# Turning du, Q and dO by crossbar DMAs instead of on TensorE, with other loads, lags and a reordered end, in a gated attention and FFN gradient

## The chip, the cores and the metric

The kernel runs on one core of one Trainium2 chip. The metric is the device time of one execution in microseconds, and less is better. An "engine" below is one of the core's units: TensorE (PE, with its weight loads listed as PEld), VectorE (DVE), ScalarE (ACT), GpSimd (POOL) and SyncE (SP), which here does nothing but issue DMAs. A "crossbar DMA" is a DMA that writes its data transposed (`dma_start_transpose`).

## The reference

One layer mixes sliding-window attention and a ReLU-gated feed-forward block with a gate per row; the kernel must give its output and the gradients with respect to everything but the feed-forward input. The forward pass, cut to what matters:

```python
# S = 2048 rows, D = 512, 32 heads of 16, window W = 256, F = 1376, all bf16
g = sigmoid((x * gate_w).sum(-1, keepdims=True))
q, k, v = split(x @ wqkv)                      # heads of 16
p = softmax(where(0 <= i - j < 256, q @ k.T / 4, -1e9))
a = (p @ v) @ wo
gate = B_x @ W_gate; gate = gate * (gate > 0)
h = gate * (B_x @ W_up)
b = h @ W_down
out = g * a + (1 - g) * b
# returned: out and, for a given grad_out, the gradients
# of x, wqkv, wo, W_gate, W_up, W_down and gate_w
# (B_x holds the same numbers as x and gets no gradient of its own)
```

## The kernel before

Rows are handled in tiles of 128 (16 of them) and in groups of four tiles (512 rows, index `tg`). Transposed copies, with features on the partitions, have names in T (`hT`, `dgT`, `duT`, `QT`, `dOT`, `KT`, `VT`); row copies have names in `_r` or `rows`. There are three stages.

**Feed-forward stage.** 44 steps run over 11 feature chunks `fc` times 4 row groups `tg`. One turn n of the loop issues `gate` and `up` of step n (matmuls `gps` and `ups`, from which `rg`, `upm` and `hT` come), `dh` of step n-1 (matmul `dhps`, from which `dgT` and `duT` come), then the turns: `turn_h` of step n-1 and `turn_dg` of step n-2 as crossbar DMAs on SP's queue, `turn_du` of step n-3 as four TensorE transposes into PSUM (`ptu`) and a DVE copy; `keep` of step n-3 stores `hT`, `dgT` and `duT` to DRAM from ACT's queue; `weights` of step n-4 multiplies the turned tiles into the weight gradients `wps` and `dps`. The first four turns also turn x (`turn_x`), compute the gate column (`gate_col`), scale grad_out into `db_r` (`db_rows`, four DVE operations per group) and turn that into `db_T` (`turn_db`), on which `dh` depends. Group loads of grad_out, `go_in`, are issued on POOL's queue with two buffers, so the third and fourth wait for `db_rows` of the first two.

**Attention stage.** The order is written out by hand (`manual_schedule`). Units of work run over 4 chunks `c` of 8 heads, 16 row tiles `j`, up to three key tiles `kb` and two halves of four heads: 360 units, one per slot n. In a slot, `front` issues two matmuls for unit n (scores `ST`, and `dPT`, the gradient of the probabilities), Exp on ACT and the mask on POOL, then `gradp` forms `Pd` on DVE; `rowsum` and `flip` handle unit n-2. A flip transposes `Pu` and `Pd`: for units on the diagonal (a third of them, tile `PP`) by a crossbar DMA `p<-PP` on SP's queue, for all others by eight TensorE transposes. Then come pieces of older work (`cd_piece`, which reads the flipped `p`) and, when a running credit of TensorE time allows, `project_parts` of the next row group (matmuls for Q, dO, K, V; `tr_rows`, which turns `QT` and `dOT` into `rows` by TensorE transposes `ptp` and two DVE copies, the first scaled; `tr_kv`, the same for K and V), and background work. SP's queue also carries `spread` and `gather` (`z_d<-QT`, `z<-z_d`: the block-structured operand of the next scores), the turns of weight matrices through DRAM (`wt`), loads `dar` of the attention's output gradient, and the stores of the gradients of q, k, v and of O (`spill`: four DMAs into `dqkv_d` and `O_d`). After the last unit the remaining slots drain what is left; at the end of the stage the operands of the next one are loaded (`early_group`, `late_weights`, `load_group(0)`).

**Final stage.** 16 row tiles: 11 matmuls for b, 4 for a, 22 and 12 for dx (lines L912, L915 and L919), plus one for the gradient of gate_w; a tile's dx is stored by a DMA on POOL's queue.

Within one engine's queue instructions run in the order in which they are written; DMAs on one issuing engine are issued in that order too.

Of the kernel before, what the change touches and what calls it, by code (L numbers as in the profile page):

```python
# [22 lines left out]
def kernel(  # L23
# [64 lines left out]
    dqkv_d = dram.tile([S, 3 * D], BF, name="dqkv_d")  # L88
    O_d = dram.tile([S, D], BF, name="O_d")
# [33 lines left out]
    with ExitStack() as p1, tc.manual_schedule():  # L123
# [25 lines left out]
        nc.sync.dma_start(x_r[:, 0:TPG, :], rows_of(x_d, 0))  # L149
# [4 lines left out]
        load_go(0)  # L154
        load_go(1)
# [3 lines left out]
        nc.scalar.dma_start(Wg_sb[:, :, W0:F], Wg_v[:, :, W0:F])  # L159
        nc.scalar.dma_start(Wu_sb[:, :, W0:F], Wu_v[:, :, W0:F])  # L160
# [24 lines left out]
        def db_rows(tg):  # L185
            for k in range(TPG):
                t = tg * TPG + k
                nc.vector.tensor_scalar(db_r[:, t, :], go_in[tg][:, k, :], omg_all[:, t:t + 1], None, op0=ALU.mult)
            if tg + 2 < NTG:
                load_go(tg + 2)  # L190
# [72 lines left out]
        def dh(k):  # L263
# [4 lines left out]
            k.dgT, k.duT = tile1("dgT"), tile1("duT")  # L268
            nc.vector.tensor_tensor(out=k.dgT[:], in0=dh_sb[:], in1=k.upm[:], op=ALU.mult)
            nc.gpsimd.tensor_tensor(out=k.duT[:], in0=dh_sb[:], in1=k.rg[:], op=ALU.mult)  # L270

        def turn_h(k):
            k.h_r = fp.tile([P, TPG, P], BF, tag="h_r", name="h_r")
            nc.sync.dma_start_transpose(out=k.h_r[:], in_=k.hT[:])

        def turn_dg(k):
            k.dgu_r = fp.tile([P, 2, TPG, P], BF, tag="dgu_r", name="dgu_r")
            nc.sync.dma_start_transpose(out=k.dgu_r[:, 0, :, :], in_=k.dgT[:])

        def turn_du(k):  # L280
            pt = ps1.tile([P, TPG, P], BF, tag="tr", bufs=2, name="ptu")
            for t in range(TPG):
                nc.tensor.transpose(pt[:, t, :], k.duT[:, t * P:(t + 1) * P], ident[:])
# [36 lines left out]
        for n in range(N1 + 6):  # L320
# [47 lines left out]
    if True:  # L368
        st = p3.enter_context(tc.tile_pool(name="attst", bufs=2))
        gwp = p3.enter_context(tc.tile_pool(name="gwp", bufs=2))  # L370
        p3b = ExitStack()
        wq = p3b.enter_context(tc.tile_pool(name="wq", bufs=1))
# [3 lines left out]
        zt = [wq.tile([P, 2, HG, 2 * P], BF, name=f"z{i}") for i in range(ZB)]  # L376
# [8 lines left out]
        def project_parts(c, tg):  # L385
# [25 lines left out]
            def tr_rows():  # L411
                rows = pj.tile([P, 2, TPG, P], BF, tag="rows", name="rows")
                pt = tr("Q", "dO")
                nc.vector.tensor_scalar(rows[:, 0, :, :], pt[:, 0, :, :], scale, None, op0=ALU.mult)
                nc.vector.tensor_copy(rows[:, 1, :, :], pt[:, 1, :, :])
                t4["rows"] = rows

            def tr_kv():
# [3 lines left out]
                for a, lo, eng in ((0, 0, "dve"), (1, 17, "dve")):  # L422
# [3 lines left out]
            return [lambda: mm("Q", 0, "dve"), lambda: mm("dO", 3, "dve"), lambda: mm("K", 1, "dve"),  # L426
                    lambda: mm("V", 2, "dve"), tr_rows, tr_kv]
# [18 lines left out]
        def cd_piece(c, kb, qb, half, last):  # L446
# [12 lines left out]
            if last:  # L459
                nc.scalar.copy(sts[c][0][:, kb, 1:3, :].rearrange("p a (h d) -> p h a d", h=HG),  # L460
# [504 lines left out]
```

## Time and profile before

| what | value |
|---|---|
| median of three runs | 1039.25 us (1038.76 to 1042.58) |
| profiled execution | 1040.05 us, span 1038.3 us |
| mean granted TensorE clock | 0.986 |
| instructions of PE | 11852 matmuls, 982.8 us busy (95% of the span) |
| DVE, ACT, POOL busy | 55%, 46%, 45% |
| DMA traffic | 162.85 MB in 393335 packets, of which 293297 are under 512 B |
| feed-forward stage | 0 to about 283 us |
| attention stage | about 283 to 855 us |
| final stage | about 855 us to the end |

A profile is one execution; its times are microseconds unless marked ns. A row of the timeline gives start, duration, engine, line, operation, the tile written and the tiles read, and in brackets how long the engine stood idle before it and what it then waited for. A row of windows gives the length of a stretch and the busy time of each engine in it, then the granted clock, the mean busy share of the 16 DMA engines and GB/s. Matmuls overlap: a matmul of 128x512 shows 0.38 us, while in an unbroken stream the next one starts 0.22 us after it. So a busy PE need not be a PE at its best, and what a matmul costs is read from the distance between starts.

### The profile page before, as it was taken

The page shows a single profiled execution, that of the slowest core. Times are in us where ns is not written, and L with a number is a line of the kernel's source. Part 1 is how long each engine was busy: PE and PEld are TensorE (multiplying, and loading weights), DVE is VectorE, ACT ScalarE, POOL GpSimd, SP SyncE. Part 2 cuts the span into 40 slices and gives each one's busy share as a digit, 9 for nine tenths or more (in the row PEclk, how much of TensorE's full clock was granted, in tenths as well). Part 3 has the DMA queues.
Part 4 walks back from the last instruction along what each step waited for, and adds up shares of the span by engine and source line. Part 5 has one row for each costly group of instructions (what it writes and reads, how often), then busy time and mean ns, then how long its engine had stood idle before and what let it go on. Part 6 is the DMA issues. An engine that isn't in the chain of part 4 may idle for free.

```text
span 1038.3 us, 28954 instructions
## 1 busy us (share of the span) xinstructions
PE 982.8 (95%) x11852; PEld 634.0 (61%) x11852; DVE 569.8 (55%) x1101; ACT 481.1 (46%) x808; POOL 466.4 (45%) x810
## 2 busy tenths in 40 slices
PE   5799999999989999999999999999999769999997
PEld 3466666566647777677776777766777534444443
DVE  3344444333268888767788677886777502322222
ACT  3323333222147777666677676666667411001000
POOL 2355544344345556655556455565555411211211
PEclk9999999999999999999999999999999879999999
DMA  9557676866555676787767776569869989667740
GB/s 303 90 148 178 179 178 169 205 160 142 136 114 102 123 145 117 154 168 149 143 119 149 163 161 127 132 118 177 143 97 231 266 222 260 158 154 179 187 107 21
DMA packets 393335, 162.85 MB, mean 157 GB/s; under 512 B 293297, under 2 KB 388818, under 8 KB 393202
## 3 DMA queue, kind: packets, MB, share of 16 engines
q1 hardware_dynamic: 368306, 131.30, 60.6%
q10 hardware_dynamic: 21648, 20.13, 6.2%
q0 software_dynamic: 3248, 9.57, 3.0%
q8 instruction: 93, 1.52, 0.6%
q14 instruction: 40, 0.33, 0.1%
HBM read 54.36 MB, written 48.10 MB: 99 GB/s over the span
## 4 chain that ended last, share of the span: by engine, by line
PE 82%; DMA 7%; issue 3%; DVE 3%; ACT 2%; SPq 1%; POOL 1%; ACTq 0%; POOLq 0%; DVEq 0%
PE pt L647 9%; PE wps L298 7%; PE dPT L598 7%; PE ST L596 7%; PE gps L247 4%; PE bps L883 4%; PE dhps L247 4%; PE CD L454 4%; PE dxps L919 3%; PE BA L624 3%; PE dps L300 3%; PE pp L395 3%; PE ups L247 3%; PE dxps L912 3%; PE dxps L915 3%; PE wps L540 3%
## 5 line engine op out<-in xcount | busy, mean ns | idle before, releaser
L615 DVE TENSOR_TENSOR Pd<-Pu,dPT 128x512 bf16<-128x512 bf16 x232 | 158.3, 684 | 55.2 <-POOL Pu L609 34.1
L604 ACT ACTIVATE Pu<-ST 128x512 bf16<-128x512 f32 x232 | 139.5, 601 | 59.2 <-PE ST L596 53.2
L606 POOL TENSOR_SCALAR_AFFINE_SELECT PP<-PP 128x512 bf16<-128x512 bf16 x128 | 81.1, 634 | 160.7 <-ACT PP L604 160.1
L598 PE MATMUL dPT<-z,VT 128*128 128x512 bf16 x360 | 136.5, 379 | 4.1 <-DVE Pd L615 1.6
L596 PE MATMUL ST<-z,KT 128*128 128x512 bf16 x360 | 136.3, 379 | 0.8 <-DMA z<-z_d 0.8
L75 ACT COPY p<-pt 128x1024 bf16<-128x1024 bf16 x116 | 117.4, 1012 | 30.7 <-PE pt L647 30.3
L454 PE MATMUL CD<-rq,p 128*128 128x32 bf16 x1440 | 117.0, 177 | 7.9 <-DMA p<-PP 6.4
L457 PE MATMUL CD<-rq,p 128*128 128x16 bf16 x1440 | 113.7, 169 | 0.0
L261 POOL TENSOR_TENSOR hT<-rg,upm 128x512 bf16<-128x512 bf16 x44 | 50.5, 1148 | 134.5 <-DVE upm L259 114.0
L298 PE MATMUL wps<-dgu_r,x_r 128*128 128x256 bf16 x704 | 106.8, 275 | 2.1 <-DVE wst L77 2.0
L604 ACT ACTIVATE PP<-ST 128x512 bf16<-128x512 f32 x128 | 76.7, 600 | 55.0 <-PE ST L596 48.2
L454 PEld LDWEIGHTS <-p 128*128 128x128 bf16 x1440 | 95.8, 96 | 6.7 <-DMA p<-PP 6.7
L609 POOL TENSOR_SCALAR_AFFINE_SELECT Pu<-Pu 128x512 bf16<-128x512 bf16 x112 | 71.1, 634 | 56.3 <-ACT Pu L604 54.7
L77 DVE COPY p<-pt 128x1024 bf16<-128x1024 bf16 x116 | 79.7, 687 | 28.3 <-PE pt L647 26.8
L615 DVE TENSOR_TENSOR PP<-PP,dPT 128x512 bf16<-128x512 bf16 x128 | 86.6, 677 | 9.9 <-POOL PP L606 9.8
L624 PEld LDWEIGHTS <-Pu 128*128 128x128 bf16 x928 | 68.0, 96 | 37.3 <-issue 10.3
L647 PE MATMUL pt<-ident,Pd 128*128 128x128 bf16 x928 | 90.2, 220 | 0.0
L457 PEld LDWEIGHTS <-p 128*128 128x128 bf16 x1440 | 89.0, 96 | 1.7 <-issue 1.7
L647 PE MATMUL pt<-ident,Pu 128*128 128x128 bf16 x928 | 89.3, 218 | 0.0
L298 PEld LDWEIGHTS <-x_r 128*128 128x128 bf16 x704 | 67.6, 99 | 24.4 <-issue 3.2
L259 DVE SCALAR_TENSOR_TENSOR upm<-rg,ups 128x512 bf16<-128x512 bf16 x44 | 30.2, 687 | 94.0 <-PE ups L247 91.9
L624 PE MATMUL BA<-KV,Pu 128*128 128x33 bf16 x928 | 77.5, 178 | 4.5 <-ACT BAs L630 3.9
(136 smaller groups left out, 2073.8 us busy)
## 6 DMA issues: line engine op xcount, KB each, us to landing
z<-z_d SPq DMA_DIRECT2D x128, 64.0 KB
dar<-da_d SPq DMA_DIRECT2D x28, 256.0 KB
hT_d<-hT ACTq DMA_DIRECT2D x44, 128.0 KB
dgT_d<-dgT ACTq DMA_DIRECT2D x44, 128.0 KB
duT_d<-duT ACTq DMA_DIRECT2D x44, 128.0 KB
dqkv_d<-dqkv_st SPq DMA_DIRECT2D x21, 256.0 KB
hT_g<-hT_d SPq DMA_DIRECT2D x8, 640.0 KB
dgT_g<-dgT_d SPq DMA_DIRECT2D x8, 640.0 KB
```

Source lines behind the costliest of these rows:

```text
L75: nc.scalar.copy(out, in_)
L247: nc.tensor.matmul(out[:], lhsT=w(c), rhs=x(c), start=(c == 0), stop=(c == DC - 1))
L298: nc.tensor.matmul(acc["w"][:, c, :], lhsT=x_r[:, t, c * P:(c + 1) * P], rhs=k.dgu_r[:, :, i, :], start=(go_ and c % 2 == 0), stop=no_, sk ...
L454: nc.tensor.matmul(cd[0][:, h, :], lhsT=p2[:, 0, hh, :], rhs=rq[:, h, 0:2 * Dh], start=cd[1], stop=True, skip_group_check=True)
L457: nc.tensor.matmul(cd[0][:, h, 0:Dh], lhsT=p2[:, 1, hh, :], rhs=rq[:, h, 2 * Dh:3 * Dh], start=False, stop=True, skip_group_check=True)
L596: nc.tensor.matmul(ST[:], lhsT=KTt[:, ksl], rhs=zt[zb][:, 0, hsl, (jl % 2) * P:(jl % 2 + 1) * P], start=True, stop=True)
L598: nc.tensor.matmul(u.dPT[:], lhsT=VTt[:, ksl], rhs=zt[zb][:, 1, hsl, (jl % 2) * P:(jl % 2 + 1) * P], start=True, stop=True)
L604: nc.scalar.activation(u.Pu[:], ST[:], ACT.Exp, scale=scale)
L606: nc.gpsimd.affine_select(out=u.Pu[:], in_=u.Pu[:], compare_op=ALU.is_ge, fill=0.0, base=0, pattern=[[0, HH], [1, P]], channel_multiplier=-1)
L615: nc.vector.tensor_tensor(out=u.Pd[:], in0=u.Pu[:], in1=u.dPT[:], op=ALU.mult)
L624: nc.tensor.matmul(BA[:, h, 0:33], lhsT=u.Pu[:, hh, :], rhs=kv[:, u.kb % TPG, h, :], start=(u.first and hh == 0), stop=True, skip_group_ch ...
L647: nc.tensor.transpose(pt[:, a, hh, :], src[:, hh, :], ident[:])
```

## The change

The edits, by place:

- **Start.** The first x group is loaded in two halves; all four `go_in` loads are issued at once; the rest of W_gate and W_up is loaded from SP's queue, behind x and the first part of W_down, no longer from ACT's; the sigmoid is called once at the start on a zeroed column; half of `db_rows` moves from DVE to ACT.
- **Feed-forward stage.** `dgT` and `duT` lie in one tile `dgu`, and one crossbar DMA turns both (`turn_dgu`, step n-4). `turn_du` with its TensorE transposes and DVE copy is gone. `dh` goes from lag 1 to lag 2, the stores of `dgT` and `duT` from lag 3 to 4, `weights` from lag 4 to 6, and the loop runs two turns longer.
- **Attention stage.** `tr_rows` issues two crossbar DMAs on SP's queue; the scale goes into two later operations, one of them an added DVE operation per row tile. The `KT` and `VT` copies out of PSUM move from DVE to ACT. The `dPT` matmul leaves `front` and is issued after the slot's row sums and flips (`front_dp`); row sums and TensorE flips go from lag 2 to lag 3, with a fourth `Pu` and `Pd` buffer. The last four diagonal units are flipped on TensorE. The first group projects Q and dO, spreads and gathers, and only then projects K and V.
- **End of attention.** One DRAM tile `dqkvo_d` takes the place of `dqkv_d` and `O_d`, so that a spill is one DMA; the first `hT` and `dgT` tiles of the final stage are loaded into the two z tiles as these come free; the gradient pieces of the last chunk are partly issued in the draining slots; late weights are due ten slots earlier.
- **Final stage.** All W_gate matmuls of a tile come before its W_up ones; the matmul and store of gate_w's gradient precede the last twelve matmuls; the last dx tile is stored from SP's queue instead of POOL's.

The core of the diff:

```diff
-            go_in[tg] = fp.tile([P, TPG, D], BF, tag="go_in", bufs=2, name="go_in")
+            go_in[tg] = fp.tile([P, TPG, D], BF, tag="go_in", bufs=NTG, name="go_in")
...
+        nc.vector.memset(g_all[:, 0:1], 0.0)
+        nc.scalar.activation(g_all[:, 0:1], g_all[:, 0:1], ACT.Sigmoid)
...
-        nc.scalar.dma_start(Wg_sb[:, :, W0:F], Wg_v[:, :, W0:F])
-        nc.scalar.dma_start(Wu_sb[:, :, W0:F], Wu_v[:, :, W0:F])
+        nc.sync.dma_start(Wg_sb[:, :, W0:F], Wg_v[:, :, W0:F])
+        nc.sync.dma_start(Wu_sb[:, :, W0:F], Wu_v[:, :, W0:F])
...
-        def turn_dg(k):
+        def turn_dgu(k):
             k.dgu_r = fp.tile([P, 2, TPG, P], BF, tag="dgu_r", name="dgu_r")
-            nc.sync.dma_start_transpose(out=k.dgu_r[:, 0, :, :], in_=k.dgT[:])
-
-        def turn_du(k):
-            pt = ps1.tile([P, TPG, P], BF, tag="tr", bufs=2, name="ptu")
-            for t in range(TPG):
-                nc.tensor.transpose(pt[:, t, :], k.duT[:, t * P:(t + 1) * P], ident[:])
-            evac(k.dgu_r[:, 1, :, :], pt[:], "dve")
+            nc.sync.dma_start_transpose(out=k.dgu_r[:].rearrange("p a t f -> p (a t) f"),
+                                        in_=k.dgu[:].rearrange("p a s -> p (a s)"))
...
+            if at(2):
+                dh(at(2))
             if at(1):
-                dh(at(1))
                 turn_h(at(1))
...
             if at(4):
-                f = weights(at(4))
+                turn_dgu(at(4))
+                keep(at(4), (dgT_d, at(4).dgT), (duT_d, at(4).duT))
+            if at(6):
+                f = weights(at(6))
...
             def tr_rows():
                 rows = pj.tile([P, 2, TPG, P], BF, tag="rows", name="rows")
-                pt = tr("Q", "dO")
-                nc.vector.tensor_scalar(rows[:, 0, :, :], pt[:, 0, :, :], scale, None, op0=ALU.mult)
-                nc.vector.tensor_copy(rows[:, 1, :, :], pt[:, 1, :, :])
+                for i, nm in enumerate(("Q", "dO")):
+                    nc.sync.dma_start_transpose(out=rows[:, i, :, :], in_=t4[nm][:])
...
-            for a in range(3):
-                eng.dma_start(dqkv_d[rsl, a * D + c * P:a * D + (c + 1) * P].rearrange("(t p) n -> p t n", p=P),
-                                  dqkv_st[:, tsl, a, :])
-            eng.dma_start(O_d[rsl, c * P:(c + 1) * P].rearrange("(t p) n -> p t n", p=P), O_st[:, tsl, :])
+            eng.dma_start(dqkvo_d[t0 * P:(t0 + NT // 2) * P, c * 4 * P:(c + 1) * 4 * P].rearrange("(t p) n -> p t n", p=P),
+                          sts[c][:, tsl, :, :].rearrange("p t a n -> p t (a n)"))
...
+                        u.dma = u.role == "d" and (c < DC - 1 or j < NT - 2)
...
-                if 2 <= n < NU + 2:
-                    w = units[n - 2]
+                if 2 <= n < NU + 2 and units[n - 2].dma:
+                    flip(units[n - 2])
+                if LAG <= n < NU + LAG:
+                    w = units[n - LAG]
                     rowsum(w)
-                    flip(w)
+                    if not w.dma:
+                        flip(w)
...
+                if u is not None:
+                    front_dp(u)
...
-                    nc.gpsimd.dma_start(dx_d[tsl, :], dx_sb[:])
+                    (nc.sync if t == NT - 1 else nc.gpsimd).dma_start(dx_d[tsl, :], dx_sb[:])
```

How SP's queue reads in the steady part of the feed-forward stage, one step and the start of the next, before. Each row is one DMA with its line, destination, source and shape; `da_d` is the store of a scaled grad_out tile that another part of the loop issues.

```order
L274 DMA_TRANSPOSE h_r<-hT 128x4x128
L278 DMA_TRANSPOSE dgu_r<-dgT 128x4x128
L312 DMA out_dram<-wst 128x4x128
L313 DMA out_dram<-wst 128x4x128
L314 DMA out_dram<-dst 128x512
L210 DMA da_d<-da_t 128x512
```

And with the change:

```order
L279 DMA_TRANSPOSE h_r<-hT 128x4x128
L283 DMA_TRANSPOSE dgu_r<-dgu 128x8x128
L312 DMA out_dram<-wst 128x4x128
L313 DMA out_dram<-wst 128x4x128
L314 DMA out_dram<-dst 128x512
L214 DMA da_d<-da_t 128x512
```

The number of DMAs per step is the same; the second turns eight blocks of 128x128 instead of four.

SP's queue in the attention stage, around the spreading and gathering of one row group, before (`p` is a flipped diagonal unit, `wt` and `WgT_d` the turn of W_gate, `z` and `z_d` the operand of the next scores):

```order
L638 DMA_TRANSPOSE p_4976<-PP 128x8x128
L436 DMA z_3431<-z_d_67 32x2x512 x4
L503 DMA_TRANSPOSE wt<-in_B_W_gate_dram 128x512
L432 DMA z_d_68<-QT 8x16x256
L432 DMA z_d_68<-dOT 8x16x256
L638 DMA_TRANSPOSE p_5115<-PP 128x8x128
L432 DMA z_d_69<-QT 8x16x256
L432 DMA z_d_69<-dOT 8x16x256
L507 DMA WgT_d<-wt 128x512
L638 DMA_TRANSPOSE p_5227<-PP 128x8x128
L638 DMA_TRANSPOSE p_5362<-PP 128x8x128
```

And with the change:

```order
L432 DMA z_d_67<-QT 8x16x256
L432 DMA z_d_67<-dOT 8x16x256
L646 DMA_TRANSPOSE p_4756<-PP 128x8x128
L432 DMA z_d_68<-QT 8x16x256
L432 DMA z_d_68<-dOT 8x16x256
L503 DMA WgT_d<-wt 128x512
L646 DMA_TRANSPOSE p_4871<-PP 128x8x128
L415 DMA_TRANSPOSE rows<-QT 128x4x128
L415 DMA_TRANSPOSE rows<-dOT 128x4x128
L646 DMA_TRANSPOSE p_4996<-PP 128x8x128
L499 DMA_TRANSPOSE wt<-in_B_W_gate_dram 128x512
```

Two crossbar DMAs stand between two flips, after the spreads of the same row group; each following flip stands behind them.

SP's queue at the end of the attention stage, before:

```order
L709 DMA_TRANSPOSE early_a<-dqkv_d 128x4x256
L490 DMA Wd_sb_16524<-in_B_W_down_dram 128x10x512
L492 DMA Wd_sb_16524<-in_B_W_down_dram 96x512
L638 DMA_TRANSPOSE p_17360<-PP 128x8x128
L709 DMA_TRANSPOSE early_a<-O_d 128x4x256
L638 DMA_TRANSPOSE p_17471<-PP 128x8x128
L638 DMA_TRANSPOSE p_17567<-PP 128x8x128
L726 DMA hT_g<-hT_d 128x10x256
L728 DMA hT_g<-hT_d 96x256
L730 DMA go_g<-in_grad_out_dram 128x2x512
L726 DMA dgT_g<-dgT_d 128x10x256
```

And with the change:

```order
L488 DMA Wd_sb_15790<-in_B_W_down_dram 96x512
L718 DMA_TRANSPOSE early<-dqkvo_d 128x4x256
L646 DMA_TRANSPOSE p_16649<-PP 128x8x128
L718 DMA_TRANSPOSE early<-dqkvo_d 128x4x256
L646 DMA_TRANSPOSE p_16755<-PP 128x8x128
L718 DMA_TRANSPOSE early<-dqkvo_d 128x4x256
L723 DMA f_16813<-hT_d 128x10x256
L725 DMA f_16813<-hT_d 96x256
L718 DMA_TRANSPOSE early<-dqkvo_d 128x4x256
L723 DMA f_17266<-dgT_d 128x10x256
L725 DMA f_17266<-dgT_d 96x256
```

The load of W_down now stands ahead of the early crossbar DMAs, the last flip on SP's queue ahead of the loads of `hT` and `dgT` (here `f`), and no flip stands behind them.

More of the change, by code (lines that the diff above doesn't have):

```diff
@@ L87 @@
     duT_d = dram.tile([F, S], BF, name="duT_d")
-    dqkv_d = dram.tile([S, 3 * D], BF, name="dqkv_d")
-    O_d = dram.tile([S, D], BF, name="O_d")
+    dqkvo_d = dram.tile([S, 4 * D], BF, name="dqkvo_d")
     da_d = dram.tile([S, D], BF, name="da_d")
@@ L375 @@
         ZB = 2
-        zt = [wq.tile([P, 2, HG, 2 * P], BF, name=f"z{i}") for i in range(ZB)]
+        zt = [wq.tile([P, 2, HG, 2 * P], BF, tag=f"z{i}", name=f"z{i}") for i in range(ZB)]
         for i in range(ZB):
@@ L532, in piece @@
             def piece(part, t0, first, last):
-                dqkv_st, O_st = sts[c]
                 if first:
-                    hold["w"] = ps.tile([P, 3, P] if part < DC else [P, D], F32, tag="M", bufs=4, name="wps")
-                wps = hold["w"]
+                    tag, bufs = ("TR", 2) if part == DC and rest is not None else ("M", 4)
+                    hold[part] = ps.tile([P, 3, P] if part < DC else [P, D], F32, tag=tag, bufs=bufs, name="wps")
+                wps = hold[part]
                 for t in range(t0, t0 + 4):
@@ L539, in piece @@
                     if part < DC:
-                        nc.tensor.matmul(wps[:], lhsT=x_r[:, t, part * P:(part + 1) * P], rhs=dqkv_st[:, t, :, :],
+                        nc.tensor.matmul(wps[:], lhsT=x_r[:, t, part * P:(part + 1) * P], rhs=sts[c][:, t, 0:3, :],
                                          start=go_, stop=no_)
                     else:
-                        nc.tensor.matmul(wps[:], lhsT=O_st[:, t, :], rhs=rows[t], start=go_, stop=no_)
+                        nc.tensor.matmul(wps[:], lhsT=sts[c][:, t, 3, :], rhs=rows[t], start=go_, stop=no_)
                 if not last:
@@ L546, in piece @@
                 if part < DC:
-                    ws = gwp.tile([P, 3, P], BF, tag="ws", name="ws")
-                    evac(ws[:], wps[:], "act")
+                    ws = (gwp if rest is None else S2["t6"]).tile([P, 3, P], BF, tag="ws", bufs=2 if rest is None else 5, name="ws")
+                    evac(ws[:], wps[:], "act" if rest is None or part % 2 else "dve")
                     return store(part, ws)
@@ L565, in grad_parts @@
             else:
-                parts = [(p, 0, NT) for p in range(DC)] + [(DC, 0, NT)]
+                for a, b in ((0, NT - 4), (NT - 4, NT)):
+                    if a:
+                        out += [(DC, t0, t0 == 0, t0 + 4 == NT) for t0 in range(0, NT, 4)]
+                    out += [(p, t0, t0 == 0, t0 + 4 == NT) for p in range(DC) for t0 in range(a, b, 4)]
+                return [lambda a=a: piece(*a) for a in out]
             for part, a, b in parts:
@@ L739 @@
+            for f in parts[:2]:
                 f()
@@ L743 @@
                 gather(*groups[0], pr)
+            for f in parts[2:]:
+                f()
             ahead = project_parts(*groups[1])
@@ L789 @@
                     front(u)
+                    if u.last and gi + 1 == len(groups) and u.j % TPG in (1, 3):
+                        ev.setdefault(n + 2, []).append(("dma", lambda i=(u.j % TPG) // 2: early_f(i)))
                     if u.last and u.j % TPG in (1, 3) and gi + 1 < len(groups):
@@ L836 @@
                     credit -= 0.65
[L837 removed]
+                if u is not None and u.c == DC - 1 and not bgq and u.j >= TPG and "T0" not in S2:
                     early = early_group()
@@ L854 @@
             grp_next = load_group(0)
-            for f, more in S2["grads"]:
+            for f in S2["grads"]:
                 store = f()
@@ L924 @@
                         nc.tensor.matmul(dgw_ps[:], lhsT=pdz[:], rhs=x_r5[:, pt_, :], start=(pt_ == 0), stop=False)
+                    if t == NT - 1:
+                        nc.tensor.matmul(dgw_ps[:], lhsT=dz_bf[:], rhs=x_r5[:, t, :], start=False, stop=True)
+                        dgw_sb = t6.tile([1, D], BF, tag="dgw_sb")
+                        nc.scalar.copy(dgw_sb[:], dgw_ps[:])
+                        nc.sync.dma_start(out_7.rearrange("(o d) -> o d", o=1), dgw_sb[:])
                     pending_dgw = (t, dz_bf)
+                    for cc in range(C3):
+                        nc.tensor.matmul(dxps[:], lhsT=T_g[:, 4 * (cc % DC) + cc // DC, lsl], rhs=wqkvT_sb[:, cc, :],
+                                         start=(i == 0), stop=(i == nmm - 1))
+                        i += 1
                     dx_sb = t6.tile([P, D], BF, tag="dx_sb")
```

186 lines of the change are left out of this document (96 added, 90 removed).

## The prediction

> **What bounds the kernel now.** I read the page's totals first, then its stages by windows, then the waits inside the stages that are not full.
>
> ```profile
> span 1038.3 us, 28954 instructions
> PE 982.8 (95%) x11852; PEld 634.0 (61%) x11852; DVE 569.8 (55%) x1101; ACT 481.1 (46%) x808; POOL 466.4 (45%) x810
> ```
>
> PE is busy 95% of the span and no other engine reaches 60%. The windows tell where the other 5% lie. Columns after the window are its length, the busy time of each engine, the granted clock, the mean share of the DMA engines and GB/s.
>
> ```profile
> 0.00:30.00 30.00, 16.79 (x176) 11.61 (x176) 10.15 (x20) 11.96 (x16) 9.74 (x15) 1.00 1.06 274
> 30.00:60.00 30.00, 23.28 (x171) 13.86 (x172) 11.60 (x25) 8.26 (x14) 10.31 (x9) 0.94 0.39 97
> 100.00:200.00 100.00, 100.00 (x708) 63.11 (x705) 41.44 (x69) 34.94 (x61) 48.30 (x47) 1.00 0.72 178
> 280.00:300.00 20.00, 15.78 (x109) 8.35 (x107) 11.00 (x20) 4.01 (x6) 5.18 (x6) 1.00 0.28 80
> 800.00:840.00 40.00, 26.12 (x491) 19.64 (x490) 17.09 (x34) 16.81 (x30) 17.18 (x37) 0.77 1.08 232
> 900.00:950.00 50.00, 50.00 (x229) 21.87 (x228) 13.85 (x30) 5.87 (x10) 10.62 (x15) 1.00 0.74 183
> sum 506.00, PE 498.79 PEld 363.14 DVE 388.36 ACT 355.09 POOL 287.76; mean PE 124.70 PEld 90.79 DVE 97.09 ACT 88.77 POOL 71.94
> ```
>
> The last row sums four windows that cover 300 to 806 us, the body of attention: 7.2 us idle in 506. The feed-forward stage and the final stage are full. So two things can shorten this kernel: taking instructions off PE in the full stretches, which pays in full, and closing the holes, which are the first 60 us (19.9 us idle), the start of attention (4.2), and 800 to 840 us (13.9 idle, and a clock of 0.77).
>
> **The change part by part.** The sum goes against the profiled execution, 1040.05 us (span 1038.3 and 1.75 around it); that stands 0.8 us above the median of the runs, 1039.25.
>
> *Start.* PE's waits, from the timeline:
>
> ```profile
> 5.76 1.89 PE L171 MATMUL ptx<-ident,x_r 128*128 128x128 bf16 x16 [5.76 <-DMA x_r<-in_A_x_dram]
> 17.52 0.40 PE L224 MATMUL ptw<-ident,Wd_sb 128*128 128x128 bf16 x4 [1.03 <-DMA Wd_sb<-in_B_W_down_dram]
> 24.17 1.04 PE L247 MATMUL dhps<-db_T,WdT 128*128 128x512 bf16 x4 [2.33 <-DVE db_T L77]
> 33.07 1.89 PE L247 MATMUL dhps<-db_T,WdT 128*128 128x512 bf16 x4 [3.96 <-DVE db_T L77]
> 41.11 1.04 PE L247 MATMUL dhps<-db_T,WdT 128*128 128x512 bf16 x4 [2.32 <-DVE db_T L77]
> 46.70 1.02 PE L247 MATMUL dhps<-db_T,WdT 128*128 128x512 bf16 x4 [1.10 <-ACT db_T L75]
> 8.49 1.28 ACT L75 ACT_TABLE_LOAD   x1 [8.49 <-issue]
> 19.40 11.78 DMA go_in<-in_grad_out_dram
> 31.28 1.14 DVE db_r L188 x4
> ```
>
> Four waits of `dh` for `db_T` make 9.7 us. Behind them stands a `go_in` load of 11.78 us in the chain of waits, which could not be issued before a buffer came free. With four buffers all loads start at once, and with lag 2 each `dh` has one more step of PE work ahead of it. The table load of 1.28 us leaves the path to the first `x_T`. Against that: the first 30 us already run the DMA engines at a share of 1.06, and the change puts 1 MB of grad_out earlier into them and the W_down part that `ptw` waits for behind all of x, as before, but now beside those loads. I let that cost 2 us: 9.7 + 1.3 - 2 = 9. Ends: -11 (nothing is late) and -2 (the loads only move the waits to `ptw`). Moving half of `db_rows` to ACT costs nothing: ACT is busy 12 of 30 us; if that cover went, 2 x 0.3 us per group, by half of the 1.14 us that four such DVE operations take in the chain (last row).
>
> *du by crossbar.* The step of the steady stage, and the DMAs that take the work over:
>
> ```profile
> 125.94 0.39 PE L283 MATMUL ptu<-ident,duT 128*128 128x128 bf16 x4
> 126.17 0.60 PE L298 MATMUL wps<-dgu_r,x_r 128*128 128x256 bf16 x4
> L278 SPq DMA_TRANSPOSE dgu_r<-dgT x44: 1191/1224/2948, 26.3 to 276.7; - x44
> L638 SPq DMA_TRANSPOSE p<-PP x128: 1231/1253/4346, 300.5 to 833.3; - x128
> q1 hardware_dynamic: 544, 0.13, 21.7%
> q1 hardware_dynamic: 765, 0.18, 66.5%
> ```
>
> Four transposes hold PE from 125.94 to 126.17, 0.23 us; 44 steps make 10.1 us, all on the path, since PE is full there. What takes their place is off PE. SP issues as many DMAs as before, and a crossbar of 128x1024 (`p<-PP`) holds its queue 1.25 us at the median, as long as one of 128x512 (1.22): no cost on SP. The 512 further packets per step cost DMA time. The first q1 row is a window of 3 us, 36 to 39, with one such DMA alone: 21.7% of it, 0.65 us of all 16 engines, 19 ns a packet. At a share of 0.72, a step of 5.42 us (the distance of `gps` in the chain of waits, below) leaves 1.52 us free; 0.65 fits, and the share in the shorter step becomes (3.90 + 0.65) / 5.19 = 0.88. The wait for the later turn is covered by `weights` at lag 6: two steps, 10.4 us, after the crossbar. The saved DVE copy is worth nothing (DVE is 41% busy). I take -10; ends 0 (crossbars late by as much as is saved) and -10.
>
> ```profile
> 50.56 0.86 PE gps L247 x4
> 55.98 0.86 PE gps L247 x4
> 199.17 6.39 DMA hT_d<-hT
> 206.96 0.89 PE L298 MATMUL wps<-dgu_r,x_r 128*128 128x256 bf16 x4 [2.02 <-DVE wst L77]
> ```
>
> Once, at 199, a store on ACT's queue holds the chain for 6.39 us and PE idles 2.02. The larger lags should absorb it: -2, ends 0 and -4 (the chain around it loses about twice the idle time recorded).
>
> [...]
>
> *Q and dO by crossbar.*
>
> ```profile
> 296.07 0.39 PE L408 MATMUL ptp<-ident,QT 128*128 128x128 bf16 x4
> 296.30 0.39 PE L408 MATMUL ptp<-ident,dOT 128*128 128x128 bf16 x4
> L598 PE MATMUL dPT<-z,VT 128*128 128x512 bf16 x360 | 136.5, 379 | 4.1 <-DVE Pd L615 1.6
> 434.04 1.25 SPq L638 DMA_TRANSPOSE p<-PP  x1
> 435.34 2.72 SPq L436 DMA_DIRECT2D z<-z_d  x4
> 438.17 1.93 SPq L638 DMA_TRANSPOSE p<-PP  x1
> 783.45 1.64 SPq L473 DMA_DIRECT2D O_d<-O_st  x1
> ```
>
> 0.23 us per four again, 32 times: -7.4 on PE; ends 0 and -7.4. On SP's queue 32 crossbars of 1.25 us come in, 40 us, and 21 of the 28 spill issues go (the one shown takes 1.64 us). The first three SP rows are back to back: in such stretches each flip behind a `rows` pair comes 2.5 us later, and `cd_piece` waits for it. The median flip is not waited for (idle by `p<-PP` below occurs only at the end), so I charge +3 for the few crowded places; ends 0 and +15, where 15 is six places of 2.5 us. Moving the K and V copies to ACT costs nothing while ACT has its 30% free (355 of 506 busy).
>
> *dPT behind the flips.* Its row records 4.1 us idle before it, for buffers of the pair it shares with `ST`. Issued later, it finds its buffer free: -4; ends 0 and -7, all idle time of the four windows. `gradp` gets `dPT` later by some 1 us, which lag 3 gives back.
>
> *Start of attention.* K and V now come while z is gathered: -1 of the 4.2 idle (0 to -3).
>
> *End of attention.*
>
> ```profile
> 806.81 15.22 DMA p<-PP x2
> 825.99 6.83 DMA p<-PP
> 833.32 4.76 DMA p<-PP
> ```
>
> The chain stands 26.8 us on three late crossbar flips, while the DMAs are saturated (1.08). The last four diagonal units go to TensorE, 8 transposes each, 0.46 us by the price above, 1.8 us together. What is late next are the loads of the final stage, which remain in number though they are issued earlier and into free tiles. Of 13.9 us idle, and some 6 lost to the clock (0.23 of 26), I take -15 + 1.8 = -13; ends -5 (loads late instead) and -20.
>
> *Tail.*
>
> ```profile
> 1031.12 0.75 DVE L927 SCALAR_TENSOR_TENSOR dx_sb<-gw_b,dz,dxps 128x512 bf16<-128x512 bf16 x1 [2.21 <-PE dxps L919]
> L960 POOLq DRAIN  x3: 45/102/5333, 1032.1 to 1038.0; - x3
> ```
>
> From the last dx tile at 1031.9, 6.4 us pass to the end, 5.33 of them in POOL's drain behind its last store. A store on SP need not wait for that drain: -2.5; ends 0 and -4.
>
> Sum: -9 - 10 - 2 - 7.4 + 3 - 4 - 1 - 13 - 2.5 = -46, so 994 for a profiled run and 993 for the median. All low ends together give -66, 973; all high ends +8, 1047, but they are separate places and will not fall together.
>
> **The rivals.**
>
> 1. *SP's queue becomes the bound in attention.* For it: the back-to-back rows, and each flip now stands behind two more DMAs. Against it: only the last flips are waited for today. If half of the 32 crossbars come onto the path at 1.25 us, that is +20 in place of +3: 1010. All of them: 1030.
> 2. *The start gains nothing,* since PE waits for `ptw` or `gw_col` behind all loads (share 1.06): +8, so 1001.
> 3. *The end gives nothing back,* since the DMAs stay saturated there (1.08): the loads take the flips' place and 8 of 13 us stay, 1001.
> 4. *Slower: the crossbars bind the feed-forward stage.* The second q1 row, 24 to 31 us, has 765 packets in 66.5% of 7 us, 97 ns each, beside POOL's loads. At that price 1536 packets per step take 9.3 us of 16 engines, with 2.7 of other traffic (3.90 less 1024 x 19 ns / 16): 12.0 per step against 5.42, +290, less 36 from the other parts: 1293. It decides from 37 ns a packet, where the step is 6.2 us and eats the other gains. Against it: in 100 to 200 us the same mix, grad_out loads included, holds a share of 0.72.
> 5. *The transposes were hidden anyway:* then du and rows are worth 0, and 1010 results. PE's 100.00 of 100 us speaks against it.
>
> **How the numbers follow.** My forecast, with terms in their ranges, 0.66; rival 1 0.11; rival 2 or 3, 0.13; rival 4 0.05; rival 5 0.05. I predict 993. The low end is that of all terms, 973, since gains in separate places do add up. The high end takes in rivals 1, 2, 3 and 5, and two of them at once (993 + 17 + 8): 1020. What is left out is rival 4, rival 1 in full, and gains beyond my ends. About 0.5%, 5 us, is what a measurement of this kernel can tell from no change: faster than that 0.91, within it 0.03 (rival 1 in full with others), slower 0.06.
>
> **What would show it.** Right: no `ptu` or `ptp` of Q and dO on PE; feed-forward steps 5.19 us apart with a DMA share near 0.88; no wait of `dhps` for `db_T`; no `p<-PP` of many us at the end of the chain; the end under 5 us after the last dx tile. Wrong: PE idle before `wps` for `dgu_r` (du), before `CD` for `p` or `rq` for `rows` (SP's queue), a wait on `Wd_sb` near 17 us longer than 1.03 (start), or `bps` waiting for loads (end). The forecast falls if the feed-forward step stays at 5.42, or if attention's windows show more idle time than 7 us in 506.

## The result, and the profile after

| | median | range | ratio to before |
|---|---|---|---|
| before | 1039.15 us | 1038.76 to 1042.58 | |
| changed | 1014.79 us | 1010.26 to 1016.59 | 0.9752 (0.9712 to 0.9792) |

The change makes the kernel 24.4 us faster. The forecast was 46 us, 993: the direction and the range held, the size did not. It lies in the range because the high end, 1020, was set to take in the rivals. The profiled execution of the changed kernel took 1013.56 us. Its page:

```profile
span 1010.6 us, 28410 instructions
PE 963.2 (95%) x11580; PEld 620.1 (61%) x11580; DVE 527.7 (52%) x1053; ACT 503.0 (50%) x849; POOL 462.4 (46%) x806
```

PE issues 272 matmuls fewer, as the change says (176 for du and 128 for Q and dO are gone, 32 for the last flips are new), and is still 95% busy: span and work shrank together. Where the 27.7 us of span went is read from two marks in the chain of waits, the last weight gradient stored by the feed-forward stage and the first matmul of the final stage. Before:

```profile
286.52 1.98 DMA out_dram<-dst
...
855.80 2.54 PE bps L883 x11
```

After:

```profile
55.59 0.86 PE ups L251 x4
60.79 0.86 PE ups L251 x4
...
265.92 1.97 DMA out_dram<-dst
...
830.29 2.54 PE bps L917 x11
```

| stage | before | after | difference | forecast |
|---|---|---|---|---|
| feed-forward, to the first mark | 286.5 | 265.9 | -20.6 | -9 - 10 - 2 = -21 |
| attention, between the marks | 569.3 | 564.4 | -4.9 | -7.4 + 3 - 4 - 1 - 13 = -22.4 |
| final stage, to the end of the span | 182.5 | 180.3 | -2.2 | -2.5 |

The feed-forward stage came out as worked out, with its steps 5.20 us apart, and so did the end. All that is missing, 17 us, is missing in attention. One trace carries its own scatter: a second trace of the changed kernel gives -18.1, -5.5 and -2.2 for these three rows, and in nine traces with this feed-forward code the first mark lies between 265.4 and 270.1 us. Windows of the changed kernel; the last row sums four that cover 300 to 780 us:

```profile
0.00:30.00 30.00, 18.72 (x198) 12.44 (x199) 11.33 (x20) 14.93 (x23) 8.67 (x15) 1.00 0.98 296
30.00:60.00 30.00, 29.53 (x207) 17.71 (x204) 12.07 (x20) 12.09 (x22) 18.86 (x17) 1.00 0.75 167
60.00:100.00 40.00, 40.00 (x269) 24.69 (x268) 17.46 (x24) 15.86 (x28) 21.58 (x23) 1.00 1.00 211
265.00:290.00 25.00, 15.63 (x131) 7.77 (x132) 10.98 (x20) 10.01 (x16) 6.54 (x12) 0.98 0.44 103
290.00:296.00 6.00, 5.71 (x61) 3.79 (x60) 3.80 (x9) 3.45 (x7) 4.44 (x11) 0.52 0.60 126
780.00:820.00 40.00, 32.84 (x554) 24.84 (x553) 21.02 (x45) 20.42 (x34) 17.43 (x38) 0.91 1.09 253
sum 480.00, PE 471.80 PEld 344.62 DVE 344.19 ACT 350.87 POOL 271.86; mean PE 117.95 PEld 86.16 DVE 86.05 ACT 87.72 POOL 67.97
```

The first 60 us lost their holes (48.3 us busy, 40.1 before). The body of attention idles 8.2 us in 480, more than the 7.2 in 506 before, which is the sign that the forecast named for its fall. The start of attention has a hole of 9.4 us in 25, and in the 6 us behind it the granted clock is 0.52, so that eight transposes take 0.86 us there and 0.47 behind it. From 780 to 820 there is still a hole of 7.2, with the DMA engines at 1.09.

Three places in the changed kernel show what stands in them. SP's queue at the start of attention, from the timeline, and the PE wait that follows:

```profile
277.00 2.09 SPq L415 DMA_TRANSPOSE rows<-QT  x1
279.14 1.26 SPq L415 DMA_TRANSPOSE rows<-dOT  x1
...
283.11 1.20 SPq L415 DMA_TRANSPOSE rows<-QT  x1
284.35 1.26 SPq L415 DMA_TRANSPOSE rows<-dOT  x1
285.71 5.38 SPq L646 DMA_TRANSPOSE p<-PP  x4
...
289.68 0.59 PE L597 MATMUL ST<-z,KT 128*128 128x512 bf16 x1 [5.55 <-ACT PP L603]
```

```profile
285.71 3.24 DMA p<-PP
```

Four new crossbars stand ahead of the first flips. The first flip comes back 3.24 us after 285.71 (second block, from the chain), ACT's Exp gets its `PP` buffer then, and PE waits 5.55 us for ACT. From the chain at the end of attention, and PE's wait there:

```profile
781.98 1.89 SPq L488
...
784.90 7.21 DMA z<-z_d
...
792.25 0.58 PE L597 MATMUL ST<-z,KT 128*128 128x512 bf16 x1 [5.54 <-DMA z<-z_d]
```

The last gather of z stands behind the load of the turned W_up (L486 and L488), takes 7.21 us to land, and PE waits 5.54 us for it. And two groups of the body, 300 to 780 us, columns count, busy time and mean, then idle time before them:

```profile
L618 PE MATMUL dPT<-z,VT 128*128 128x512 bf16 x328 | 124.2, 379 | 0.1
L655 PE MATMUL pt<-ident,Pu 128*128 128x128 bf16 x848 | 81.3, 217 | 3.3 <-DVE p L77 3.3
```

`dPT` no longer waits, but the TensorE flips now do, 3.3 us, for a copy on DVE.

### The profile page after: what moved, and what is told of

It is laid out like the page before. It is cut to its first block, busy times and chain, and to the rows that moved or that the text cites. A ratio compares the mean times of both kernels' runs of the same rounds, so it can differ in the third digit from the quotient of the medians.

```text
span 1010.6 us, 28410 instructions
## 1 busy us (share of the span) xinstructions
PE 963.2 (95%) x11580; PEld 620.1 (61%) x11580; DVE 527.7 (52%) x1053; ACT 503.0 (50%) x849; POOL 462.4 (46%) x806
## 4 chain that ended last, share of the span: by engine, by line
PE 78%; DMA 6%; DVE 4%; issue 4%; POOL 3%; ACT 2%; SPq 2%; POOLq 0%; ACTq 0%; DVEq 0%
PE pt L655 9%; PE dxps L947 7%; PE ST L597 7%; PE dPT L618 6%; PE wps L298 6%; PE wps L536 4%; PE dxps L960 4%; PE bps L917 4%; PE pp L396 3%; PE BA L632 3%; PE dhps L251 3%; PE CD L454 3%; PE ups L251 3%; PE gps L251 3%; PE dps L300 3%
## 5 line engine op out<-in xcount | busy, mean ns | idle before, releaser
L623 DVE TENSOR_TENSOR Pd<-Pu,dPT 128x512 bf16<-128x512 bf16 x232 | 155.8, 682 | 23.9 <-PE dPT L618 11.7
L75 ACT COPY p<-pt 128x1024 bf16<-128x1024 bf16 x118 | 119.5, 1013 | 12.2 <-PE pt L655 9.3
L457 PEld LDWEIGHTS <-p 128*128 128x128 bf16 x1440 | 88.9, 96 | 41.2 <-issue 1.6
L454 PEld LDWEIGHTS <-p 128*128 128x128 bf16 x1440 | 104.0, 96 | 0.9 <-issue 0.3
L924 ACT COPY a_sb<-aps 128x512 f32<-128x512 f32 x16 | 9.4, 586 | 150.5 <-issue 137.6
```

The lines of the kernel that those rows point to most:

```text
L75: nc.scalar.copy(out, in_)
L454: nc.tensor.matmul(cd[0][:, h, :], lhsT=p2[:, 0, hh, :], rhs=rq[:, h, 0:2 * Dh], start=cd[1], stop=True, skip_group_check=True)
L457: nc.tensor.matmul(cd[0][:, h, 0:Dh], lhsT=p2[:, 1, hh, :], rhs=rq[:, h, 2 * Dh:3 * Dh], start=False, stop=True, skip_group_check=True)
L623: nc.vector.tensor_tensor(out=u.Pd[:], in0=u.Pu[:], in1=u.dPT[:], op=ALU.mult)
```

## The experiments

Two theories were set against each other for the missing 17 us. One: new crossbars hold SP's queue, and flips, gathers and `dar` loads behind them come late. Two: PE's waits in attention are set by ACT, DVE and full DMA engines, and only change places. Ratios are to the kernel before on the same chip, and 0.001 is 1.04 us. The changed kernel was measured twice: 0.9752 at first, 0.9776 beside the three experiments that follow it below. These three are compared with 0.9776, all later ones with the mean, 0.9764. The two measurements lie 2.5 us apart, so a difference of that size shows nothing.

### The changed kernel again

> The changed kernel once more, as the common reference of this group. Both theories: 1010 to 1017 us, as in its four runs so far, whose median is 1014.8.

1015.41 us, ratio 0.9776 (0.9757 to 0.9796).

### Rows of the first two groups on TensorE

```diff
-                for i, nm in enumerate(("Q", "dO")):
-                    nc.sync.dma_start_transpose(out=rows[:, i, :, :], in_=t4[nm][:])
+                if (c, tg) in groups[:2]:
+                    pt = tr("Q", "dO")   # copied into rows by two DVE copies
+                else:
+                    ...
```

> The changed kernel, but the rows of Q and dO of the first two row groups are turned on TensorE again; the other 14 groups keep their crossbar DMAs. Theory 1 (order on SP's queue): four crossbar DMAs stand ahead of the first flips there, and PE's idle time of 5.55 us before ST at 289.68, which came after them, goes away: -5.6 + 2 groups x 2 x 0.23 = -4.7 us, about 1010. Theory 2 (the wait is for ACT's Exp and its PP buffers in any case, since the first units are all short rows): PE pays 0.9 us and gains nothing, about 1016.

1009.53 us, ratio 0.9732 (0.9710 to 0.9753): 4.6 us faster than the changed kernel beside it, close to theory 1's 4.7. The wait of 5.55 us is gone; no wait in 270 to 296 us is longer than 1.23. Four crossbars in a place where nothing covers them cost 5.5 us of waits, and the slow clock behind them, for 0.9 saved on PE: in this run the granted clock is 1.00 from 270 to 300 us.

### The last gather from ACT's queue

```diff
+            eng = nc.scalar if (c, tg, pr) == (DC - 1, NTG - 1, 1) else nc.sync
...
-                nc.sync.dma_start(zt[pr][2 * Dh * k:...
+                eng.dma_start(zt[pr][2 * Dh * k:...
```

> The changed kernel, but the last gather of z (four DMAs) is issued from ACT's queue instead of SP's, so that it does not stand behind the loads of W_gate and W_up in one queue. Theory 1 (order on the queue): the stop of PE at 786.5, 5.7 us before the next ST, goes away, and 2 of them come back at the loads of the final stage: -4, about 1011. Theory 2 (the DMA engines themselves are full there, share 1.09): the gather lands as late as before: within 1.5 us of the changed kernel.

1013.05 us, ratio 0.9753 (0.9732 to 0.9775): 2.4 us below the changed kernel, with overlapping intervals, so no gain is shown. The chain of this run at the same place:

```profile
774.52 9.08 DMA p<-PP
...
787.41 7.75 DMA p<-PP
```

The gather no longer ends the wait; two flips do, which take 9 and 8 us behind the loads of W_gate and W_up. Getting one transfer past the loads leaves the next one behind them.

### Rows of all groups on TensorE

> The changed kernel, but the rows of Q and dO are turned on TensorE in all 16 groups, as before the change, without the scaling. Theory 1 (the crossbars' place on SP's queue costs about what they save): +7.4 on PE, -5.6 at the start of attention, -1 to -3 in its body: -1 to +1, 1013 to 1016. Theory 2 (the crossbars are free outside, and the missing time has another cause): +7, about 1022.

1006.91 us, ratio 0.9688 (0.9666 to 0.9709): 9.1 us faster than the changed kernel beside it. Neither theory had that: it undoes the "Q and dO by crossbar" part of the change (the scale stays where the change put it, and the TensorE credit charged for this piece goes back from 0.1 to 0.44), puts 7.4 us of transposes back on PE, and gains. The same queue and the same group as above, in this run, and its window of 780 to 820 us:

```profile
281.96 5.42 SPq L647 DMA_TRANSPOSE p<-PP  x4
```

```profile
L656 PE MATMUL pt<-ident,Pu 128*128 128x128 bf16 x848 | 81.2, 217 | 0.0
```

```profile
780.00:820.00 40.00, 35.67 (x580) 26.07 (x578) 17.45 (x39) 18.88 (x32) 16.50 (x35) 0.96 1.12 271
```

The first flips are issued 3.8 us earlier (6.0 earlier counted from the first mark, which lies at 268.2 here), the flips' wait for DVE is 0 instead of 3.3, and PE is busy 2.8 us longer in 780 to 820 (3.1 longer in the last 60 us before the final stage). So the crossbars of Q and dO cost some 16.5 us (9.1 + 7.4) for 7.4 saved. In 300 to 780 us they neither win nor lose: both kernels get through the same other work there, 8168 matmuls with crossbars and 8276 without, of which 112 are the added transposes. PE's wait for `dar` in that stretch is 2.9 us in both.

### du on TensorE again

```diff
-            nc.sync.dma_start_transpose(out=k.dgu_r[:].rearrange("p a t f -> p (a t) f"),
-                                        in_=k.dgu[:].rearrange("p a s -> p (a s)"))
+            nc.sync.dma_start_transpose(out=k.dgu_r[:, 0, :, :], in_=k.dgT)
+            ...  # four transposes of duT into ptu, and a DVE copy
```

> The changed kernel, but du is turned on TensorE again (four transposes and a DVE copy at lag 4, then weights at lag 6), and the crossbar DMA turns dg alone. Theory 1 (the transposes lay on the path and the crossbar is hidden by the two steps of lag): steps of the feed-forward stage 5.42 us apart instead of 5.20, +10, about 1025, with the DMA share of 60 to 100 us back from 1.00 to some 0.8. Theory 2 (the full DMA engines cost the stage elsewhere): less than +6, below 1021.

1022.34 us, ratio 0.9845 (0.9821 to 0.9869): +0.0081 against 0.9764, 8.4 us. Theory 1 in kind, a little below its 10. The DMA share falls as expected:

```profile
60.00:100.00 40.00, 40.00 (x287) 25.39 (x286) 18.37 (x31) 14.93 (x26) 21.40 (x23) 1.00 0.79 185
```

### dPT next to ST again

```diff
                     front(u)
+                    front_dp(u)
...
-                if u is not None:
-                    front_dp(u)
```

> The changed kernel, but the dPT matmul directly follows ST again, as before the change; row sums and flips stay at lag 3. Theory 1 (the wait of dPT for its buffer was real and its removal was worth 4 to 7 us): +4 to +7, about 1020. Theory 2 (the removed waits only came back in front of ST and of the flips' PSUM tile): 0 to +2, 1015 to 1017.

1025.44 us, ratio 0.9875 (0.9854 to 0.9896): +0.0111, 11.5 us, more than either theory. In 300 to 780 us the wait stands where it was before the change, and larger:

```profile
L618 PE MATMUL dPT<-z,VT 128*128 128x512 bf16 x321 | 121.3, 378 | 9.8 <-ACT PP L603 5.6 <-DVE PP L623 2.0 <-DVE Pd L623 1.6
```

With flips and row sums at lag 3, `dPT` in front waits 9.8 us in the body. Undoing this part costs more than the 4 us forecast; but it is measured against flips at lag 3, and what lag 3 costs or saves by itself was not run.

### Rows by crossbar, alone in the kernel before

> The kernel before, with nothing changed but the rows of Q and dO turned by two crossbar DMAs on SP's queue, the scale folded into a small DVE operation per row tile. Theory 1 (their place on SP's queue ahead of the flips costs about what they save, 7.4 us): within 4 us of the kernel before. Theory 2 (they only hurt together with the other edits of the attention stage): -6 to -8, about 1032.

1058.18 us, ratio 1.0185 (1.0163 to 1.0206): 19 us slower than the kernel before, far outside both theories, on theory 1's side. Its chain has the crossbars in it by name (L414), with the `dar` load behind them:

```profile
436.06 1.27 SPq L414
437.38 2.31 SPq L414
441.89 4.40 DMA dar<-da_d
```

The same happens at 573 and 711 us: once per chunk, where `dar` is loaded, SP's queue is what the kernel waits for. PE waits 8.2 us before the matmuls that read `dar` in 320 to 800 us, where it waited 0.4 before the edit. The rest of the 19 us is not traced here, and this run still charges the turn as TensorE work in its credit.

### Rows on TensorE, and the late loads in pieces

```diff
-            return [lambda p=p: load(*p) for p in pairs]
+            ...  # one DMA per four chunks of 128 rows, at most 512 KB
...
-                if u is None or n % 5 == 2:
+                if u is None or n % 2 == 0:
                     if late:
```

> The changed kernel with the rows of Q and dO on TensorE in all groups, and with the late loads of the final stage's weights cut into pieces of at most 512 KB, one piece every second slot instead of a whole matrix every fifth, so that no flip or gather stands behind more than a few of them. Against the kernel with rows on TensorE alone (ratio 0.9688 to the kernel before). Theory 1 (the stop of 3.6 us before ST at 781 comes from the gather standing behind 1.3 MB loads): -3 to -5, ratio 0.965. Theory 2 (the DMA engines are simply full from 755 to 830 us, whatever the order): within 2 us.

1002.98 us, ratio 0.9656 (0.9635 to 0.9677): 3.3 us below the kernel with rows on TensorE alone, in theory 1's range, but the two intervals overlap (0.9666 to 0.9709) and the runs are from different chips, so a gain in time is not shown.

```profile
780.00:820.00 40.00, 36.79 (x653) 27.59 (x650) 21.17 (x47) 21.87 (x37) 18.93 (x40) 1.00 1.09 248
```

The mechanism of theory 1 is shown: PE's wait for the last gather, 5.5 us in the changed kernel and 3.5 with rows on TensorE, is gone. At the same DMA share of 1.09, PE is busy 36.8 us here against 32.8 in the changed kernel (35.7 with rows on TensorE), and its clock stays at 1.00 instead of 0.91 (0.96): the order of the transfers matters, not only their sum. Yet between the two marks attention takes 554.4 us in this trace as in that of rows on TensorE. This version has the lowest median of all, 36 us below the kernel before.

### One crossbar for Q and dO together

```diff
-                for i, nm in enumerate(("Q", "dO")):
-                    nc.sync.dma_start_transpose(out=rows[:, i, :, :], in_=t4[nm][:])
+                nc.sync.dma_start_transpose(out=rows[:].rearrange("p a t f -> p (a t) f"),
+                                            in_=t4["QdO"][:].rearrange("p a s -> p (a s)"))
```

> The changed kernel, but QT and dOT of a row group lie in one tile, which one crossbar DMA of 128x1024 turns, in place of two of 128x512. Theory 1 (what costs is the time for which these DMAs hold SP's queue ahead of flips, gathers and dar loads; one of 128x1024 holds it 1.25 us, two of 128x512 2.5): half of the 8.5 us that the crossbars cost against TensorE comes back, -4, about 1011. Theory 2 (the load on the DMA engines, or the wait for rows itself): the same bytes, within 1.5 us of the changed kernel, 1014 to 1016.

1008.11 us, ratio 0.9726 (0.9704 to 0.9747): 0.0038 below 0.9764, 4 us, theory 1's number.

```profile
L418 SPq DMA_TRANSPOSE rows<-QdO x16: 1238/1329/2007, 276.5 to 748.6; - x16
```

The bytes are the same, the time on SP's queue is half: 16 x 1.33 us instead of 32 x 1.27. This separates the queue from the DMA engines, and speaks for the queue, though the interval overlaps with that of the changed kernel's first measurement (0.9712 to 0.9792). The traces say where: PE's wait of 5.55 us at the start of attention is 1.89 here, while the idle time in 300 to 780 us is 8.2 us in both. Counted from the first mark, the first flip is issued after 19.8 us in the changed kernel, 17.1 here and 13.8 with the first two groups or all of them on TensorE; attention between the marks takes 564.4, 559.4, 555.5 and 554.4 us.

### Rows from ACT's queue

```diff
-                    nc.sync.dma_start_transpose(out=rows[:, i, :, :], in_=t4[nm][:])
+                    nc.scalar.dma_start_transpose(out=rows[:, i, :, :], in_=t4[nm][:])
```

> The changed kernel, but the two crossbar DMAs of rows are issued from ACT's queue instead of SP's. Theory 1 (SP's queue): flips, gathers and dar loads have SP's queue as if rows were on TensorE, and PE saves the transposes: -8 to -14, less what ACT loses by holding its own queue 2.5 us per row group, up to +6 where Exp waits for it: 1003 to 1012. Theory 2 (load on the DMA engines): the same bytes, no gain: 1014 to 1021.

1085.53 us, ratio 1.0461 (1.0424 to 1.0498): 72 us slower than the changed kernel, which no theory had. From the timeline of ACT and of SP at one such pair:

```profile
352.15 1.21 ACTq L415 DMA_TRANSPOSE rows<-QT  x1
353.45 1.23 ACTq L415 DMA_TRANSPOSE rows<-dOT  x1
354.73 0.60 ACT L603 ACTIVATE Pu<-ST 128x512 bf16<-128x512 f32 x1 [5.64 <-DMA rows<-QT]
```

```profile
347.97 10.92 SPq L646 DMA_TRANSPOSE p<-PP  x2
```

ACT stands still 5.64 us, from 349.1, of which the two issues are 2.5: before them it waits. By the recorded waits the turns of the two queues wait for each other: SP's flips record 15 waits for `rows<-dOT`, 56.6 us in all, and four for `rows<-QT`, 15.6, where the changed kernel has none. ACT's Exp records five stops like the one shown, 26.0 us, and nine more without a named cause, 45.2. Why they wait, no run shows. With these waits in it, the run says nothing on the two theories.

### dh one step after gate and up again

```diff
-            if at(2):
-                dh(at(2))
             if at(1):
+                dh(at(1))
                 turn_h(at(1))
```

> The changed kernel, but dh comes one step after gate and up again, as before the change, with all of its new loads at the start. Theory 1 (the start was won by the lag, which gives db_T one more step of PE work to hide behind): the four waits of dh for db_T, 9.7 us before the change, come back in part: +4 to +8, about 1021. Theory 2 (the start was won by the loads: all go_in issued at once, the table load out of the way): 0 to +2.

1023.83 us, ratio 0.9877 (0.9855 to 0.9899): +0.0113, 11.7 us. Theory 1, and above its range. PE's waits are back where they were, four of them with 6.8 us together (9.7 before the change):

```profile
25.40 1.02 PE L251 MATMUL dhps<-db_T,WdT 128*128 128x512 bf16 x4 [1.90 <-ACT db_T L75]
32.23 1.02 PE L251 MATMUL dhps<-db_T,WdT 128*128 128x512 bf16 x4 [1.90 <-ACT db_T L75]
38.17 1.02 PE L251 MATMUL dhps<-db_T,WdT 128*128 128x512 bf16 x4 [1.90 <-ACT db_T L75]
...
43.52 1.02 PE L251 MATMUL dhps<-db_T,WdT 128*128 128x512 bf16 x4 [1.10 <-ACT db_T L75]
```

In its first 60 us PE is busy 43.2 us, where it was 40.1 before and is 48.3 in the changed kernel. So the new start without the lag wins some 3 of these 8 us, and the lag the rest. The first mark lies at 276.9 us, 8.5 to 11.0 later than in the two traces of the changed kernel, so the loss is in this stage. What the lag wins without the new loads was not run.

### du by crossbar, alone in the kernel before

```diff
-            pt = ps1.tile([P, TPG, P], BF, tag="tr", bufs=2, name="ptu")
-            ...
-            evac(k.dgu_r[:, 1, :, :], pt[:], "dve")
+            nc.sync.dma_start_transpose(out=k.dgu_r[:, 1, :, :], in_=k.duT[:])
```

> The kernel before, with nothing changed but du turned by a crossbar DMA of its own (128x512, on SP's queue right where the four TensorE transposes and the DVE copy stood, at lag 3, one step ahead of weights); all lags and loads stay. Theory 1 (the gain of du needs no more than taking the transposes off a full PE): what undoing it cost in the changed kernel, about -8, 1030. Theory 2 (it needs the longer lags: the crossbar lands up to 3.5 us after its issue, behind another on the queue, and weights and the stores wait for it): -2 or slower, 1036 and above.

1054.98 us, ratio 1.0182 (1.0157 to 1.0207): 19 us slower than before, theory 2 and worse. A window of its feed-forward stage, and two of PE's waits in it:

```profile
100.00:200.00 100.00, 90.22 (x579) 53.95 (x578) 35.76 (x48) 31.59 (x57) 44.20 (x42) 0.98 0.83 181
```

```profile
102.98 1.04 PE L295 MATMUL wps<-dgu_r,x_r 128*128 128x256 bf16 x4 [2.47 <-DMA dgu_r<-duT]
128.40 0.61 PE L295 MATMUL wps<-dgu_r,x_r 128*128 128x256 bf16 x4 [1.80 <-DMA dgu_r<-duT]
```

PE, which was busy 100.00 of these 100 us, is busy 90.22 and waits for the turned tile: from 60 to 290 us 12 waits with 14.5 us. In the changed kernel, with two steps between turn and use, no wait for `dgu_r` is recorded from 60 to 262 us. The two differ in more than the steps: this run has three crossbars per step in place of two, and which of these makes du late was not separated.

## Why the prediction was right, and where it failed

- **Start, -9: right, though the reason was weighed the wrong way.** PE is busy 8.2 us longer in the first 60 us. Undoing the lag alone costs 11.7 us, and of the 8.2 the loads, which I named first, win some 3 without it. The fear of late loads came true in part: PE waits 3.46 us for x at 13 us, which it did not before, and 1.25 instead of 1.03 for W_down.
- **du, -10: right, 8.4 when undone.** The cover that I named, two steps between turn and use, held: no wait for the turned tile is recorded. With one step, and a crossbar of its own, the edit costs 19 us. I had set the DMA share at 0.88; it became 1.00. Of the changed kernel and of the kernel before, 60 to 100 us:

```profile
q1 hardware_dynamic: 14726, 4.58, 59.1%
```

```profile
q1 hardware_dynamic: 10447, 3.11, 35.6%
```

  That is 25.7 ns a packet (59.1% of 40 us of 16 engines) against 21.8, where I had 19 from one crossbar alone in a window. Rival 4 had that mechanism; its point, 37 ns, was not reached.
- **The stop at 199, -2: wrong.** The changed kernel has the same stop, PE waiting for the copy of the finished weight gradient (`wst`): 3.3 us in two waits from 60 to 262 us, where it was 2.0 in one. The longer is the row below; its chain goes back over a transfer of 6.00 us (`woT_sb`) and two issues on ACT's queue, so the larger lags did not absorb it.

```profile
194.38 0.60 PE L298 MATMUL wps<-dgu_r,x_r 128*128 128x256 bf16 x4 [2.14 <-DVE wst L77]
```

- **Q and dO by crossbar, -7.4 + 3: wrong, and the step that failed.** Taken out of the changed kernel it gains 9.1 us, so the part is worth about +9 there (and +19 alone in the kernel before). The contention that I priced at +3, with ends of 0 and +15, came to some 16.5 (9.1 + 7.4), at the high end. I took the value near the low one, from "the median flip is not waited for" and "the few crowded places". What was missed is the first use: at the start of attention nothing lies ahead of the first flips to cover four crossbars, PE waits 5.55 us and then runs at a clock of 0.52. By the times this is 4.6 us of the 9.1; by the traces, 8.9 of 10.0 between the marks. I had priced the place at -1, without these DMAs. In the body the crossbars neither win nor lose: what they save there, 6.4 us (28 x 0.23), is lost again. The `dar` loads, which I had not priced either, bear the cost in the kernel before (8.2 us of waits), but not in the changed one (2.9 us with the crossbars and without). This is the mechanism of rival 1, given 0.11 and 1010, at another place than it named.
- **dPT, -4: right in kind, the size open.** The wait before `dPT` went from 4.1 us to 0.1. Undone, with the rest of the change in place, it costs 11.5 us, since with later flips the same wait is 9.8 us. How much the move and lag 3 win together was not run.
- **Start of attention, -1: wrong.** From the first mark (265.92) to the end of PE's 5.55 us wait (289.68) the changed kernel needs 23.8 us; the crossbars of rows are why, by the run with the first two groups on TensorE.
- **End of attention, -13: too high.** The late flips left the end of the chain, as said. But the loads, moved earlier, put the last gather behind themselves (7.21 us), and 7.2 us stay idle in 780 to 820. In the last 60 us before the final stage PE idles 8.2 us, where it idled 15.7 before. Rival 3 had this mechanism. The idle time of that window falls to 4.3 us with rows on TensorE and to 3.2 with the loads split as well.
- **Tail, -2.5: right.** The last rows of the changed kernel:

```profile
1006.62 0.75 DVE L964 SCALAR_TENSOR_TENSOR dx_sb<-gw_b,dz,dxps 128x512 bf16<-128x512 bf16 x1 [3.17 <-PE dxps L960]
1007.39 0.37 SPq L966 DMA_DIRECT2D out_dram<-dx_sb  x1
```

```profile
L992 POOLq DRAIN  x3: 45/93/5733, 1001.0 to 1010.3; - x3
```

  From the last dx tile to the end 3.2 us pass instead of 6.4: POOL's drain begins at 1001.0, beside PE's last work.

Of the 17.5 us by which attention fell short, rows by crossbar are 13.5 (9.1 measured, -4.4 forecast). The other 4 were not tested apart: the end of attention is in them, with its 7.2 us idle, and what dPT and lag 3 do together; and parts that are undone one at a time, with the others in place, need not add up. How the 9.1 us of rows divide between the first two groups and the other fourteen stays open: the times say 4.6 and 4.5, with intervals of 2 us to either side of each run, and the traces put nearly all at the first two.

For du as for Q and dO the crossbar took 0.23 us per four blocks off PE by the traces. Undone, the first costs 8.4 us and the second gains 9.1: in these runs it came down to whether the queue and the steps behind the DMA had room.

## What to carry to other kernels

A transposing DMA that takes work off a full TensorE was paid here on the issuing queue (1.27 us for one of 128x512) and in latency (3.24 us from the issue of the first flip to its landing): before moving such work, list what stands behind it on that queue at each place, the first use above all, and leave steps of work between turn and use (two, of 5.20 us each, were enough here). Where others stand behind it on the queue, one large crossbar is to be preferred to two small ones: here it held the queue 1.33 us, and two of half its size 2 x 1.27. Bulk loads are worth cutting into pieces between the small transfers that someone waits for; that took a wait of 3.5 us away here, though a gain in time was not shown. Undo each part of a compound change with the others in place: here two parts that slow the old kernel by 19 us each, as they were made there, were in the faster one, and one of them was still a loss.

## What the runs showed of the hardware

- Two crossbars of 128x512 in a row hold SP's queue 2 x 1.27 us, one of 128x1024 with the same bytes 1.33.
- A packet of the feed-forward stage costs 25.7 ns at a DMA share of 1.00, 21.8 at 0.65, and 19 in a crossbar alone; at the full share the steps still ran at 5.20 us. The first two are means over all packets of the queue.
- The granted clock of 780 to 820 us fell with PE's idle time there: 0.91 with 7.2 us idle, 0.96 with 4.3, 1.00 with 3.2. Behind the stop of 5.55 us at the start of attention it was 0.52 for 6 us, and 1.00 in the run without that stop. A stop of PE can so cost more than its own length: here some 2.9 us more, an estimate from 6 us at 0.52.
